# Two buffers for the last expert's first-layer weights in the space of the q tiles, between the q transposes and the combine weights

## The chip, the core and the metric

The kernel runs on one core of one Trainium2 chip. The core has TensorE (PE, matrix products into PSUM banks), VectorE (DVE), ScalarE (ACT), GpSimd (POOL) and SyncE (SP, which here only issues transfers), an on-chip memory of 128 partitions, and 16 DMA engines that all of SP's transfers share. The metric is the device time of one execution in microseconds; a kernel's time is the median of its runs.

## The reference

An attention with 32 memory slots per head feeds a mixture of eight experts that see only 4 slots each.

```python
# attention: batch 8, heads 8, seq 576, head_dim 64, n_mem 32
a = exp(phi - max(phi, axis=2)); a = a / (sum(a, axis=2) + 1e-9)
k_m = einsum('bhsm,bhsd->bhmd', a, k)
v_m = einsum('bhsm,bhsd->bhmd', a, v)
scores = q @ k_m.transpose(0, 1, 3, 2) / sqrt(64)
attn = softmax(scores, axis=-1)              # + 1e-9 in the divisor
x = (attn @ v_m).transpose(0, 2, 1, 3).reshape(4608, 512)
# experts: D 512, E 8, 4 slots per expert, F 1024
logits = x @ moe_phi                         # 4608 x 32
d = softmax over the 4608 rows; slot_input = (d.T @ x).reshape(8, 4, 512)
for e in range(8):
    slot_out[e] = maximum(slot_input[e] @ w1[e], 0) @ w2[e]
c = softmax over the 32 slots
out = c @ slot_out.reshape(32, 512)          # 4608 x 512, float32
```

The weights w1 and w2 are 16 MiB each, the inputs q, k and v 9 MiB each, phi 4.5 MiB and the output 9 MiB.

## The kernel before

The attention goes over the batch in four pairs. For each pair phi, k, v and q are loaded, the memory slots are formed (PE, L599), q is transposed in blocks of 32 by DVE (L700, two halves for each of the two batches, four instructions a pair), scores, softmax and logits follow, and `route` adds the pair's part to the experts' inputs. After the last pair the parts are combined into `SIM` (L1000), the input of all experts.

The experts come next. A weight load is 1 MiB: 2048 floats on each of 128 partitions. `expert_in` takes two such loads of w1 for each expert and multiplies `SIM` with them (L1064), `hidden` applies the maximum with 0 to four experts at once, transposes (L1089) and copies (L1095), `expert_out` takes two loads of w2 for each expert (L1113) and adds everything up in one PSUM bank. Between the experts of the second layer `slots` makes the combine weights c of one pair of batches: a softmax, a split into two float32r parts on DVE (L1158 and L1159, two of each), transposes on PE (L1170) and copies by ACT into `cT` (L1175). At last L1199 sums the four partial sums of the bank, ACT and DVE split the sum (L1204, L1207), L1220 multiplies it with cT for 36 blocks of 128 rows, ACT (L1229) and DVE (L1231) copy the results out of PSUM, and SP stores them (L1239) in 12 transfers of 768 KB.

Where things lie: most tiles of the attention share one arena of 44288 floats a partition. The weight buffers are cut from the same arena, 19 of them (`ws`, from `W0` up), so a weight load must wait until the attention tiles under its buffer are used up. The q tiles lie outside the arena, in a region of their own (`qtile`, two buffers of 2304 floats, `qs`). After the last q transpose cT takes that region.

What sets the order: each step is entered with `add`, with its engine, an assumed cost, what it reads and writes and a priority. A planner (`Plan.order`) plays the whole program through with these costs and writes each engine's instructions in the order in which they could start; on an engine other than SP it looks a little ahead and prefers low priority numbers. A pool (`Slots`) hands out buffers as the plan frees them, and its list `below` names pools over the same addresses that must be finished first. SP works off its queue strictly in order, and a transfer that waits for its buffer holds up all behind it. Each SP transfer adds to one of eight counters in turn, so that transfer n of the queue uses counter n modulo 8; a name such as DMAHW4_49 is a wait for such a counter, and PE_49 or DVE_49 one for an engine's.

Of the kernel before, what the change touches and what calls it, by code (L numbers as in the profile page):

```python
# [252 lines left out]
def kernel(  # L253
# [27 lines left out]
    E, DM, FF = w1.shape  # L281
# [41 lines left out]
    W_SZ = 2048  # L323
# [7 lines left out]
    CT_ALL = NBP * J * P  # L331
    TOP = 10 ** 6
    top_pool = ExitStack()
    qtile = top_pool.enter_context(tc.tile_pool(name="top", bufs=1)).tile([P, CT_ALL], F32, name="top")
# [3 lines left out]
    def shaped(off, shape):  # L338
        n = 1
        for x in shape:  # L340
            n *= x
        a = arena[:, off: off + n]
        if len(shape) > 1:
            names = "abcd"[: len(shape)]
            a = a.rearrange(
                f"p ({' '.join(names)}) -> p {' '.join(names)}",
                **dict(zip(names[:-1], shape[:-1])),
            )
        return a, (off, n)

    def area(off, shape, n, below=(), fifo=False):

        size = shaped(off, shape)[1][1]
        xs = [shaped(off + i * size, shape) for i in range(n)]
        return Slots([a for a, _ in xs], [r for _, r in xs], below, fifo)

    def stack(shape, n, fifo=False):
# [32 lines left out]
    qs = Slots(  # L390
        [qtile[:, i * Q_SZ: i * Q_SZ + Q_SZ] for i in range(2)],
        [(TOP + i * Q_SZ, Q_SZ) for i in range(2)], (), True,
    )
# [62 lines left out]
    def load(dst, src, nbytes, w, pri=None):  # L456
        add(
            SP, 0.06, lambda: nc.sync.dma_start(dst(), src), w=[w],
            dma=nbytes / DMA_RATE, pri=pri,
        )  # L460
# [465 lines left out]
    for bp in range(NBP):  # L926
# [14 lines left out]
        for h in range(2):  # L941
            plan.at(bp - 0.2 + 0.4 * h)
            for g in range(2):
                qt, t, f = hs[g][h]
# [77 lines left out]
    n_ct = NBP * J // G  # L1022
    NW = (ARENA - small) // W_SZ
    W0 = ARENA - NW * W_SZ
    ws = area(W0, [W_SZ], NW, early)
    ots = area(W0, [OT_SZ], NOUT, [ws])
    ct_tile = []

    def cT_view(i):
        if not ct_tile:  # L1030
            top_pool.close()
            pool = ctx.enter_context(tc.tile_pool(name="late", bufs=1, reuse_waits="tile"))
            ct_tile.append(pool.tile([P, CT_ALL], F32R, name="cT"))
        return ct_tile[0][:, i * CT_SZ: (i + 1) * CT_SZ]

    cTs = Slots(
        [(lambda i=i: cT_view(i)) for i in range(n_ct)], [(TOP, CT_ALL)] * n_ct, [qs],
    )


# [4 lines left out]
    hT = lambda: hTb.ap.rearrange("p (x y) -> p x y", x=8)  # L1045
    add(POOL, 2.0, lambda: nc.gpsimd.memset(hTb.ap, 0.0), r=[SIM], w=[hTb])

    def load_w(src):
        t = ws.tile()
        load(lambda: t.ap.rearrange("p (a x) -> p a x", a=src.shape[1]), src, 1 << 20, t)  # L1050
        return t

# [1 line left out]

    def expert_in(e, hb):
        w1v = w1[e].rearrange("(c p) f -> p c f", p=P)
        w1b = [load_w(w1v[:, 2 * i: 2 * i + 2]) for i in range(2)]
        for i in range(2):

            def f(i=i):  # L1060
                wv = w1b[i].ap.rearrange("p (c f) -> p c f", c=2)
                for c in range(2):
                    for j in range(4):
                        nc.tensor.matmul(  # L1064
                            hb.ap[NS * j: NS * j + NS, :256],
                            SIM.ap[:, 2 * i + c, NS * e: NS * e + NS],
                            wv[:, c, 256 * j: 256 * j + 256],
                            start=(e % EG == 0 and i == 0 and c == 0),
                            stop=(e % EG == EG - 1 and i == 1 and c == 1),
                            tile_position=(0, NS * j),  # L1070
                        )

            add(PE, pe(16, NS, 256, tiles=4), f, r=[SIM, w1b[i]], w=[hb])
# [138 lines left out]
    for bp in range(NBP):  # L1212
        for j0 in range(0, J, G):
            ot = ots.tile().split(G)
            for i in range(G):
                t = bp * J + j0 + i
# [59 lines left out]
```

## Time and profile before

| what | value |
|---|---|
| runs | 223.73 us median of 3 (223.68 to 225.53) |
| profiled execution | 221.83 us, of which its span is 220.1 us |
| PE busy | 172.5 us, 78% of the span |
| DVE busy | 135.5 us, 62% |
| ACT busy | 71.4 us, 32% |
| POOL busy | 86.7 us, 39% |
| transfers of SP's queue | 76.09 MB, 91.1% of 16 engines' span |
| weight loads | 32 of 1024 KB, 9.9 us median from issue to landing |

The span counts from the first to the last instruction of the execution; times inside it start at 0. Lines such as L700 are those of the kernel before. A row of the chain of waits has a start, a length and what ran; a row of the timeline has these with shapes and count, and in brackets how long the engine stood idle ahead of it and what ended that. A row of the windows has the stretch, its length, busy time of PE, PE's weight loads, DVE, ACT and POOL, then the granted TensorE clock (1.00 is full), the mean busy share of the DMA engines and what they moved in GB/s. Busy time is an average over stages with different limits, so the table alone doesn't say which engine sets the end.

### The profile page before, as it was taken

To read this page: it belongs to the slowest core of one execution; us is meant where nothing else is said; L and a number is where in the kernel's file an instruction comes from. 1 tells how busy PE (TensorE), PEld (TensorE's weight loads), DVE (VectorE), ACT (ScalarE), POOL (GpSimd) and SP (SyncE) were. 2 spreads that over 40 slices of the span, in tenths; PEclk is the share of its full clock that TensorE was granted. 3 is DMA by queue.
4 is the path that set the end of the run, shared out by engine and by line. 5 is a ranking of instruction groups with operands and counts; after the bars stand their busy time and mean duration, and the time that the engine had idled before them with its cause. 6 is when DMAs were issued, how large, how long until landed. Compare 5 with 4: busy or idle time off the path is not lost.

```text
span 220.1 us, 5624 instructions
## 1 busy us (share of the span) xinstructions
PE 172.5 (78%) x2418; PEld 105.3 (48%) x2418; DVE 135.5 (62%) x230; ACT 71.4 (32%) x182; POOL 86.7 (39%) x85
## 2 busy tenths in 40 slices
PE   8997977695798988598988799629999975599400
PEld 6676745354564654356654387415554340065100
DVE  6825048969459999879658965499102860268500
ACT  2041234542516626337342340201002331168400
POOL 6298019596934992999623641030000000000000
PEclk9999999979699999999969999976999999769755
DMA  6999999999999999999596493999999998049997
GB/s 215 383 395 390 380 392 381 390 380 390 385 388 389 388 406 380 389 392 406 194 410 212 188 420 102 401 350 327 395 413 410 408 409 320 3 179 411 415 415 295
DMA packets 27881, 76.45 MB, mean 347 GB/s; under 512 B 1744, under 2 KB 5840, under 8 KB 27856
## 3 DMA queue, kind: packets, MB, share of 16 engines
q1 hardware_dynamic: 27856, 76.09, 91.1%
q8 instruction: 19, 0.31, 0.6%
q14 instruction: 6, 0.05, 0.1%
HBM read 66.65 MB, written 9.44 MB: 346 GB/s over the span
## 4 chain that ended last, share of the span: by engine, by line
PE 41%; DMA 22%; DVE 14%; POOL 9%; issue 5%; ACT 2%; SPq 1%; DVEq 0%; POOLq 0%
DMA top<-in_q_dram 10%; DMA arena<-in_moe_w_dram 9%; PE bank L1064 7%; PE kvbank L476 6%; PE bank L785 5%; PE scbank L716 4%; PE bank L1220 4%; PE kvbank L599 3%; DMA out_dram<-arena 3%; DVE arena L700 3%; POOL arena L774 3%; POOL arena L562 3%; PE bank L849 2%; PE kvbank L1113 2%; POOL arena L751 2%
## 5 line engine op out<-in xcount | busy, mean ns | idle before, releaser
L549 POOL TENSOR_TENSOR arena<-arena 128x1152 f32<-128x1152 f32 x8 | 21.0, 2632 | 16.0 <-ACT arena L544 13.3
L476 PE MATMUL kvbank<-ones 128*128 128x256 f32 x92 | 25.4, 419 | 2.2 <-ACT arena L622 1.1
L700 DVE STREAM_TRANSPOSE arena<-top 128x1152 f32<-128x1152 f32 x16 | 21.7, 1361 | 7.1 <-DMA top<-in_q_dram 7.1
L774 POOL TENSOR_TENSOR arena<-arena,ssm 128x576 f32<-128x576 f32 x16 | 18.5, 1162 | 15.6 <-DVE ssm L770 15.5
L562 POOL TENSOR_TENSOR arena<-arena 128x128 f32<-128x128 f32 (+2 forms) x32 | 23.4, 731 | 2.3 <-ACT arena L555 0.3
L716 PE MATMUL scbank<-arena 64*64 64x288 f32 x256 | 21.6, 433 | 3.0 <-DVE arena L730 2.5
L785 PE MATMUL bank<-arena 128*128 128x288 f32 x64 | 21.4, 464 | 2.6 <-DVE arena L777 2.6
L751 POOL TENSOR_TENSOR arena<-arena,smx 128x576 f32<-128x576 f32 x16 | 18.4, 1158 | 11.5 <-DVE smx L746 11.5
L599 PE MATMUL kvbank<-arena 64*32 64x128 f32 x1152 | 20.2, 273 | 2.2 <-issue 1.5
L476 PEld LDWEIGHTS kvbank<-ones 128*128 128x128 f32 x92 | 18.1, 207 | 6.7 <-issue 1.6
L511 DVE TENSOR_REDUCE arena<-arena 128x128 f32<-128x1152 f32 x8 | 17.0, 2138 | 5.6 <-DMA arena<-in_phi_dram 5.6
L599 PEld LDWEIGHTS kvbank<-arena 64*32 64x32 f32 x1152 | 16.2, 106 | 6.3 <-issue 3.9
L1064 PE MATMUL bank<-arena,SIM 128*32 128x256 f32 x256 | 16.4, 421 | 3.4 <-DVE SIM L1000 3.4
L1113 PE MATMUL kvbank<-arena 128*32 128x512 f32 x128 | 15.6, 598 | 2.9 <-DMA arena<-in_moe_w_dram 2.9
L730 DVE STREAM_TRANSPOSE arena<-scbank 128x576 f32<-128x576 f32 x16 | 12.2, 765 | 8.9 <-PE scbank L716 8.9
L785 PEld LDWEIGHTS bank<-arena 128*128 128x128 f32 x64 | 12.1, 206 | 8.1 <-DVE arena L777 3.8
L1220 PE MATMUL bank<-sr,cT 128*128 128x512 f32 x36 | 13.2, 505 | 3.1 <-DVE sr L1207 1.4
L1231 DVE COPY arena<-bank 128x512 f32<-128x512 f32 x18 | 11.8, 691 | 4.7 <-DMA out_dram<-arena 2.4
L777 DVE STREAM_TRANSPOSE arena<-arena 128x576 f32<-128x576 f32 x16 | 12.1, 758 | 3.8 <-POOL arena L774 3.7
L716 PEld LDWEIGHTS scbank<-arena 64*64 64x64 f32 x256 | 9.0, 137 | 10.8 <-DVE arena L730 4.5
L756 ACT ACTIVATE arena<-arena 128x576 f32<-128x576 f32 x16 | 11.0, 688 | 8.4 <-POOL arena L751 8.4
L1064 PEld LDWEIGHTS bank<-arena,SIM 128*32 128x32 f32 x256 | 8.6, 121 | 10.7 <-DVE SIM L1000 3.6
(104 smaller groups left out, 234.4 us busy)
## 6 DMA issues: line engine op xcount, KB each, us to landing
arena<-in_moe_w_dram SPq DMA_DIRECT2D x32, 1024.0 KB, 9.9
top<-in_q_dram SPq DMA_DIRECT2D x8, 1152.0 KB, 13.8
arena<-in_k_dram SPq DMA_DIRECT2D x8, 1152.0 KB, 11.2
arena<-in_v_dram SPq DMA_DIRECT2D x8, 1152.0 KB, 13.6
out_dram<-arena SPq DMA_DIRECT2D x12, 768.0 KB, 7.6
arena<-in_phi_dram SPq DMA_DIRECT2D x8, 576.0 KB, 8.7
arena<-in_moe_phi_dram SPq DMA_DIRECT2D x1, 64.0 KB, 4.8
```

The lines of the kernel that those rows point to most:

```text
L476: lambda: nc.tensor.matmul(warm.ap, ones, ones.unsqueeze(1).to_broadcast([P, 2, P]), start=True, stop=True,),
L549: lambda: nc.gpsimd.tensor_tensor(ph(), ph(), mb.ap.unsqueeze(2).to_broadcast([P, C, J, M]), op=ALU.subtract),
L562: plus = lambda o, x, y: nc.gpsimd.tensor_tensor(o, x, y, op=ALU.add)
L599: nc.tensor.matmul(acc.ap[M * c: M * c + M, a, : 2 * D], ph()[h0: h0 + HALF, c, j, :], kv()[h0: h0 + HALF, :, c, j * D: j * D + D], start= ...
L700: nc.vector.transpose(qT.ap.rearrange("p (i u y) -> p u i y", i=2, y=Y), qt.ap[:, h * QT_SZ: h * QT_SZ + QT_SZ].rearrange("p (u i x) -> p ...
L716: nc.tensor.matmul(scb.ap[HALF * g: HALF * g + HALF, a, :JY], kb[g].ap[h0: h0 + HALF, i, c].rearrange("p r m -> p (r m)"), qT[g][c // 2].a ...
L751: lambda: nc.gpsimd.tensor_tensor(exv(), exv(), bc(mx), op=ALU.subtract),
L774: lambda: nc.gpsimd.tensor_tensor(exv(), exv(), bc(sm), op=ALU.mult),
L785: nc.tensor.matmul(lp.ap[:, :JY], vpb.ap[:, h, :], aT.ap[:, a * JY: (a + 1) * JY], start=(h == 0), stop=(h == H - 1),)
L1064: nc.tensor.matmul(hb.ap[NS * j: NS * j + NS, :256], SIM.ap[:, 2 * i + c, NS * e: NS * e + NS], wv[:, c, 256 * j: 256 * j + 256], start=(e ...
L1113: nc.tensor.matmul(pacc.ap[NS * x: NS * x + NS, 0, :DM], hT()[:, 4 * t + 2 * i + j, NS * e: NS * e + NS], wv[:, j, t, :], start=(e == 0 an ...
L1220: lambda po=po, i=i, ct=cT[bp, j0]: nc.tensor.matmul(po.ap[:, :DM], ct.ap()[:, i * P: i * P + P], sr.ap, start=True, stop=True),
```

## The change

A third pool of weight buffers, `wqs`, is cut from the q region: two buffers of 2048 floats at its start, to be had once the q tiles below them are done. They are used once each, for the two w1 loads of the last expert (e = 7). `cTs` now has to wait for `wqs` besides `qs`, since cT covers the same addresses.

```diff
     ots = area(W0, [OT_SZ], NOUT, [ws])
+    wqs = Slots(
+        [qtile[:, i * W_SZ: i * W_SZ + W_SZ] for i in range(2)],
+        [(TOP + i * W_SZ, W_SZ) for i in range(2)], [qs],
+    )
     ct_tile = []
...
     cTs = Slots(
-        [(lambda i=i: cT_view(i)) for i in range(n_ct)], [(TOP, CT_ALL)] * n_ct, [qs],
+        [(lambda i=i: cT_view(i)) for i in range(n_ct)], [(TOP, CT_ALL)] * n_ct, [qs, wqs],
     )
...
-    def load_w(src):
-        t = ws.tile()
+    def load_w(src, pool=ws):
+        t = pool.tile()
         load(lambda: t.ap.rearrange("p (a x) -> p a x", a=src.shape[1]), src, 1 << 20, t)
         return t
...
-        w1b = [load_w(w1v[:, 2 * i: 2 * i + 2]) for i in range(2)]
+        w1b = [load_w(w1v[:, 2 * i: 2 * i + 2], wqs if e == E - 1 else ws) for i in range(2)]
```

The four added lines move later line numbers by four: L1064 of before is L1068 after, L1170 is L1174.

SP's queue, from its transfer number 40 on (39 and all ahead of it stand as before; arena and top are the two regions, waits in brackets). Before:

```order
L458 DMA arena_67<-in_moe_w1_dram 128x2x1024 [waits DVE_49,DMAHW0_49,PE_49,DMAHW1_49,Activation_49,Pool_49]
L458 DMA arena_67<-in_moe_w1_dram 128x2x1024 [waits DMAHW2_49]
L458 DMA arena_67<-in_moe_w1_dram 128x2x1024
L458 DMA arena_67<-in_moe_w1_dram 128x2x1024 [waits DMAHW3_49,DVE_49,PE_49]
L458 DMA arena_67<-in_moe_w1_dram 128x2x1024 [waits DVE_49,DMAHW4_49,PE_49,Activation_49]
L458 DMA arena_67<-in_moe_w1_dram 128x2x1024 [waits DMAHW5_49]
L458 DMA arena_67<-in_moe_w1_dram 128x2x1024 [waits DMAHW6_49,DVE_49,PE_49]
L458 DMA arena_67<-in_moe_w1_dram 128x2x1024 [waits DMAHW7_49,DVE_49,PE_49]
L458 DMA arena_67<-in_moe_w1_dram 128x2x1024 [waits DMAHW0_49]
L458 DMA arena_67<-in_moe_w2_dram 128x2x1024 [waits DMAHW1_49,PE_49,Pool_49]
```

The same place after:

```order
L458 DMA top_71<-in_moe_w1_dram 128x2x1024 [waits DMAHW3_49,DMAHW0_49,DVE_49]
L458 DMA arena_67<-in_moe_w1_dram 128x2x1024 [waits PE_49,DMAHW1_49,Activation_49,Pool_49]
L458 DMA arena_67<-in_moe_w1_dram 128x2x1024 [waits DMAHW2_49]
L458 DMA arena_67<-in_moe_w1_dram 128x2x1024
L458 DMA top_71<-in_moe_w1_dram 128x2x1024 [waits DMAHW4_49,DVE_49]
L458 DMA arena_67<-in_moe_w1_dram 128x2x1024 [waits DMAHW5_49,PE_49]
L458 DMA arena_67<-in_moe_w1_dram 128x2x1024 [waits DMAHW6_49,PE_49,Activation_49]
L458 DMA arena_67<-in_moe_w1_dram 128x2x1024 [waits DMAHW7_49]
L458 DMA arena_67<-in_moe_w1_dram 128x2x1024 [waits DMAHW0_49,DVE_49,PE_49]
L458 DMA arena_67<-in_moe_w2_dram 128x2x1024 [waits DMAHW1_49,DVE_49,PE_49]
L458 DMA arena_67<-in_moe_w2_dram 128x2x1024 [waits DMAHW2_49]
L458 DMA arena_67<-in_moe_w2_dram 128x2x1024 [waits DMAHW3_49,PE_49,Pool_49]
```

The two loads into the q region stand as numbers 40 and 44, each behind a wait for DVE; the arena loads keep their waits one by one, and from the second on stand two numbers further down with them (the wait for PE and POOL of number 49 is now that of 51).

PE, from the eight instructions of the second layer that follow the second block's transposes to the sum L1199 (`kvbank` is the second layer's PSUM bank, `bank_62` to `bank_64` take the transposes of combine weights). Before:

```order
L1113 MATMUL kvbank<-arena 32x512 x8
L1170 MATMUL bank_63<-ident,arena 128x128 x3
L1170 MATMUL bank_64<-ident,arena 128x128 x3
L1113 MATMUL kvbank<-arena 32x512 x4
L1170 MATMUL bank_62<-ident,arena 128x128 x3
L1113 MATMUL kvbank<-arena 32x512 x4
L1170 MATMUL bank_63<-ident,arena 128x128 x3
L1170 MATMUL bank_64<-ident,arena 128x128 x3
L1170 MATMUL bank_62<-ident,arena 128x128 x3
L1113 MATMUL kvbank<-arena 32x512 x16
L1199 MATMUL bank_63<-arena,rep 128x512
```

The same place after:

```order
L1117 MATMUL kvbank<-arena 32x512 x16
L1174 MATMUL bank_63<-ident,arena 128x128 x3
L1174 MATMUL bank_64<-ident,arena 128x128 x3
L1174 MATMUL bank_62<-ident,arena 128x128 x3
L1117 MATMUL kvbank<-arena 32x512 x8
L1174 MATMUL bank_63<-ident,arena 128x128 x3
L1174 MATMUL bank_64<-ident,arena 128x128 x3
L1174 MATMUL bank_62<-ident,arena 128x128 x3
L1117 MATMUL kvbank<-arena 32x512 x8
L1203 MATMUL bank_63<-arena,rep 128x512
```

Four of these instructions use up one weight load; ahead of the third block's transposes there are now four loads' worth in place of two, and behind the fourth block's two in place of four. In the first layer the last sixteen instructions read the region `top` in place of the arena, with no other move.

ACT, from the copies of the first layer's results to the copies into cT, waits in brackets. Before:

```order
L1080 ACTIVATE arena<-bank_62 128x256 [waits PE_49,Activation_49]
L1080 ACTIVATE arena<-bank_64 128x256 [waits PE_49]
L1175 CAST cT<-bank_63 128x384 [waits DMAHW3_49,DMAHW4_49,DVE_49,PE_49]
L1175 CAST cT<-bank_64 128x384 [waits PE_49]
L1175 CAST cT<-bank_62 128x384 [waits DVE_49,PE_49]
```

The same place after:

```order
L1084 ACTIVATE arena<-bank_62 128x256 [waits PE_49,Activation_49]
L1084 ACTIVATE arena<-bank_64 128x256 [waits PE_49]
L1179 CAST cT<-bank_63 128x384 [waits DMAHW3_49,DMAHW0_49,DMAHW4_49,DVE_49,PE_49]
L1179 CAST cT<-bank_64 128x384 [waits PE_49]
L1179 CAST cT<-bank_62 128x384 [waits DVE_49,PE_49]
```

Nothing moves on ACT; the first copy into cT has one more counter to wait for, that of the first load into the q region.

## The prediction

> **What bounds the kernel now.** I read the page's slices first, then the chain of work that ended last, then windows of the DMA share, the queue's issues and the two engines that share the stage. The slices come first.
>
> ```profile
> DMA  6999999999999999999596493999999998049997
> GB/s 215 383 395 390 380 392 381 390 380 390 385 388 389 388 406 380 389 392 406 194 410 212 188 420 102 401 350 327 395 413 410 408 409 320 3 179 411 415 415 295
> ```
>
> A slice is 5.5 us. Transfers run without a pause to about 104 us, have holes from 104 to 138 us, run nearly without a pause again to 187 us, stop, and end with the output. So there is unused transfer time ahead of a stage that is full. The chain tells whether that stage sets the end.
>
> ```profile
> 147.67 10.18 PE bank L1064 x144
> ...
> 164.39 0.86 PE kvbank L1113 x8
> ...
> 168.59 18.81 DMA arena<-in_moe_w_dram
> 187.44 1.11 PE kvbank L1113 x8
> 188.58 0.70 DVE arena L1194
> 189.41 1.76 PE bank L1199 x2
> 191.20 0.59 ACT sr L1204
> 191.82 0.70 DVE sr L1207
> 192.57 7.80 PE bank L1220 x21
> 200.37 7.29 DMA out_dram<-arena
> ```
>
> It does: the last weight load, issued at 168.59, lands at 187.40; its eight matmuls end about 188.5 and everything after hangs on them in a row. The output that follows is itself full transfer time from its first tile on, so a shift of 188.5 shifts the end by as much.
>
> The windows say how large the holes are, and the transfer rate.
>
> ```profile
> 106.00:110.00 4.00, 3.58 (x66) 2.80 (x66) 2.06 (x4) 1.69 (x7) 2.20 (x2) 1.00 0.38 125
> 110.00:116.00 6.00, 5.34 (x33) 3.39 (x33) 3.30 (x7) 2.27 (x8) 1.16 (x1) 0.72 1.01 410
> 116.00:126.00 10.00, 8.23 (x106) 3.99 (x100) 9.48 (x18) 3.05 (x8) 4.95 (x5) 1.00 0.52 179
> 126.00:134.00 8.00, 8.00 (x48) 6.60 (x47) 5.52 (x9) 2.71 (x10) 4.22 (x4) 1.00 0.93 378
> 134.00:138.00 4.00, 3.54 (x16) 2.44 (x14) 1.41 (x3) 0.00 (x0) 0.00 (x0) 1.00 0.25 51
> 164.00:182.00 18.00, 16.87 (x146) 6.80 (x142) 9.47 (x24) 5.96 (x15) 0.00 (x0) 1.00 1.03 409
> ```
>
> The last two columns are DMA share and GB/s. From 164 to 182 us the rate is 409 GB/s, so one weight load of 1 MiB (1.049 MB) takes 1.049 / 0.409 = 2.56 us. From 116 to 126 us 48% of 10 us, 4.8 us, is unused, close to two loads.
>
> The issues of weight loads show why it is unused. Columns: start, time to the end of the group, count.
>
> ```profile
> 108.07 1.39 SPq L458 DMA_DIRECT2D arena<-in_moe_w_dram  x3
> 118.49 0.37 SPq L458 DMA_DIRECT2D arena<-in_moe_w_dram  x1
> 124.03 0.88 SPq L458 DMA_DIRECT2D arena<-in_moe_w_dram  x2
> 126.20 0.37 SPq L458 DMA_DIRECT2D arena<-in_moe_w_dram  x1
> 135.83 0.88 SPq L458 DMA_DIRECT2D arena<-in_moe_w_dram  x2
> 149.67 0.37 SPq L458 DMA_DIRECT2D arena<-in_moe_w_dram  x1
> ```
>
> SP waits for arena space that the attention still uses. Numbering SP's DMAs as they stand in its queue, 40 to 42 go at 108.07, 43 at 118.49, 44 and 45 at 124.03, 46 at 126.20, 47 and 48 at 135.83. The load at 149.67 is number 52, the first that waits for an expert matmul (L1064). From 52 to 64, 13 loads are left and nothing but the transfers paces them.
>
> **The change part by part.** Nothing is added or removed: 32 weight loads before and after, the same matmuls. Two loads, the last expert's two w1 halves, get a place outside the arena, and the 12 other loads that come after them in the queue each move into the arena space that stood two numbers earlier.
>
> *When the new places are free.* The first buffer (columns 0 to 2047) lies inside the first q buffer (0 to 2303), the second (2048 to 4095) over both. q buffers are read by L700, four times for the last pair, in turn; the third and the fourth end the use.
>
> ```profile
> 107.03 1.32 DVE L700 STREAM_TRANSPOSE arena<-top 128x1152 f32<-128x1152 f32 x1
> ...
> 111.82 1.37 DVE L700 STREAM_TRANSPOSE arena<-top 128x1152 f32<-128x1152 f32 x1
> ```
>
> So the first is free at 108.35, the second at 113.19. Queued behind the first is the group that went at 108.07: it goes about 0.8 us later (0.3 of wait, one issue of 0.4 to 0.5). Nobody reads those weights before L1064 begins at 147.67, and SP has no attention load left behind them, so this costs nothing; the cover is some 25 us.
>
> *What the transfers then do.* With 2.56 us a load and about 110.8 us as the start of data: loads 40 to 43 land by 121.1, 44 (issued 113.2) by 123.6, 45 (space of 118.49) by 126.2; 46 and 47 (space of 124.03) by 131.5; 48 (space of 126.20) by 134.1, as long as the old 46 took. The two extra loads fit the hole of 116 to 126 us. From 135.83 on SP stands two loads further: the load that waits for the first expert matmul at 149.67 is number 54, and 11 are left in place of 13. The last weight lands 2 x 2.56 = 5.1 us earlier, at 182.3. That the holes are used costs other engines nothing that the trace shows: L730 takes the same beside a full and beside a half-empty DMA.
>
> ```profile
> 91.66 0.78 DVE L730 STREAM_TRANSPOSE arena<-scbank 128x576 f32<-128x576 f32 x1
> ...
> 118.50 0.78 DVE L730 STREAM_TRANSPOSE arena<-scbank 128x576 f32<-128x576 f32 x1
> ```
>
> *What is late next.* PE, by its order. These are PE's and then DVE's rows at the end of the weights stage; in brackets the idle time ahead and its releaser.
>
> ```profile
> 178.40 1.06 PE L1113 MATMUL kvbank<-arena 128*32 128x512 f32 x8
> 180.47 1.17 PE L1170 MATMUL bank<-ident,arena 128*128 128x128 f32 x9 [1.00 <-DVE arena L1159]
> 181.57 1.92 PE L1113 MATMUL kvbank<-arena 128*32 128x512 f32 x16
> 184.97 1.06 PE L1113 MATMUL kvbank<-arena 128*32 128x512 f32 x8 [1.48 <-DMA arena<-in_moe_w_dram]
> 187.44 1.06 PE L1113 MATMUL kvbank<-arena 128*32 128x512 f32 x8 [1.40 <-DMA arena<-in_moe_w_dram]
> ...
> 178.52 0.45 DVE L1158 CAST arena<-arena 128x288 fp32r<-128x288 f32 x1
> ...
> 179.86 0.46 DVE L1159 TENSOR_TENSOR arena<-arena 128x288 fp32r<-128x288 f32 x1
> ```
>
> The trace counts eight records to a load. With data there, PE idles no more for the two DMA waits (1.48 and 1.40). The 1.00 us that it waited for DVE shrinks, because the new order has one more pair of loads ahead of the third block's transposes and only two loads behind the fourth's: the four DVE steps of the fourth block (178.52 to 180.32, 1.80 us) start when the third block's transposes end, about 179.35 by the sum of PE's work, and end 181.25; PE has two loads (1.92 us) to do meanwhile and waits some 0.15. Sum: 188.50 - 1.48 - 1.40 - 1.00 + 0.15 = 184.8; the last two loads, now on end, take the 1.92 of the row above rather than 2 x 1.06, 0.2 less, and a small seam between rows goes too: 184.5. The data would allow 182.3 + 1.1 = 183.4. So 5.1 us of earlier transfers are worth 4.0, since PE's own work takes the rest. The last copies to cT of the new order need about 0.5 us of ACT behind transposes that end 182.5, before PE is done: nothing.
>
> *The clock behind it.* After the last weights L1199 sums the parts, at a reduced clock.
>
> ```profile
> 186.30:189.70 3.40, 1.35 (x9) 0.46 (x10) 0.69 (x1) 0.00 (x0) 0.00 (x0) 1.00 0.03 13
> 189.70:193.10 3.40, 2.00 (x3) 0.50 (x2) 0.69 (x1) 0.59 (x1) 0.00 (x0) 0.50 0.02 5
> ...
> 131.07 2.79 PE kvbank L476 x12
> 192.57 3.78 PE L1220 MATMUL bank<-sr,cT 128*128 128x512 f32 x8 [1.40 <-DVE sr L1207]
> ```
>
> A stretch of 3.4 us with 1.35 us of PE work at clock 1.00 was followed by one at 0.50. After the change the 3.4 us ahead of the sum hold about 2.5 us of work, since the two DMA waits are gone. How L1199 goes at clock 1.00 no row shows; from L476 at 1.00, 2.79 / 12 = 0.23 us for 256 columns, I estimate 2 x 0.47 = 0.93 for its two of 512, against 1.76 now: 0.8 less. The first output tile needs three L1220, 3.78 / 8 = 0.47 each at 0.50, 0.7 less in all if that too went at 1.00. The ends are 0 (both as now) and -1.5 (both at 1.00); I take the sum at 1.00 and L1220 as now, -0.8, for the stretch ahead of L1220 stays thin (0.9 of about 3.2 us busy), like the 1.35 above.
>
> Sum against the profiled execution: 221.83 (span 220.1) - 4.0 - 0.8 = 217.0. The median of the runs is 223.73, 1.9 above that execution; the same 4.8 off it gives **218.9 us**.
>
> **The rivals.** *The clock as now.* It drops again ahead of L1199: 223.73 - 4.0 = 219.7. For it: the waits for DVE and ACT between L1199 and L1220 remain. Against it: the 2.5 us of work ahead.
>
> *The clock stays whole to the output.* 223.73 - 4.0 - 1.5 = 218.2. By the rows it needs the thin 3.4 us before L1220 to pass unseen, which the window at 186.3 did not. The Trainium skill (TensorE: Matmul & The Clock Gate, What's actually happening) has the gate fall to half only after at least one idle window of about 3.4 us; by that rule no gap here would be long enough. This trace doesn't agree, since 0.50 came behind a stretch with 1.35 us of work in it.
>
> *The hole isn't filled.* If the loads behind 40 and 44 fell back by what the two take, 13 loads' worth would still be open at 149.67, and the end stays: 223.7; with one load of two placed, DMA bounds the end, 2.56 us off, 221.2. For it: SP's queue is in order and two new waits for DVE stand in it. Against it: they end at 108.35 and 113.19, ahead of 118.49 and 124.03, so neither is the last wait.
>
> *The transposes wait (slower).* cT is laid over the same region, and its first copy now waits for the two loads also, on counters which every eighth DMA shares.
>
> ```profile
> 168.85 0.48 ACT L1175 CAST cT<-bank 128x384 fp32r<-128x384 f32 x1 [4.00 <-PE bank L1170]
> ```
>
> Were that wait to hold for the last load on such a counter (64, landing 182.3), PE would stop at the second block's transposes at 173.0, until the copy at 182.8, and end 184.5 + 9.8 = 194.3 rather than 188.5: 223.7 + 5.8 = 229.5. It decides once the first copy starts later than about 177. Against it: the copy waits today on counters 3 and 4, and load 60, the fifth from the end on counter 4, landed only about 187.40 - 4 x 2.56 = 177.2, yet the copy ran at 168.85. The waits are for a count reached long ago.
>
> **How the numbers follow.** Forecast 0.50; the clock as now 0.18; the clock whole 0.17; the hole not filled or half filled 0.11; transposes wait 0.04. Taking the first three and the half-filled case, low is 218.2 less 1.0 for a rate and runs that spread by 1.9 us before (221.83 to 223.73), 217.2; high is the half-filled 221.2. One per cent, 2.2 us, is about what a measurement can tell from no change: faster than 221.5 are the first three and a little of the fourth, 0.87; the same 0.09; slower 0.04.
>
> **What would show it.** Right: SP's issues near 108.4 and 113.2 into `top`, DMA share near 1 from 110 to 134 us, last weight landing near 182.3, no DMA wait ahead of the last expert matmuls or one below 0.3 us, their end near 184.5, L1199 near 0.9 us, the output's first issue 4 to 5.5 us earlier. Wrong: the last weight still near 187, arena issues after 118 us later than above, attention rows that grew beside the fuller DMA, or the first copy to cT later than 177.

## The result and the profile after

| comparison | kernel before | changed kernel | ratio, 95% interval |
|---|---|---|---|
| first | 224.63 us median of 4 | 220.26 us median of 4 (216.7 to 222.0) | 0.9713 [0.9645, 0.978] |
| second (`e1_again`) | 224.75 us median of 11 | 217.55 us median of 6 (216.24 to 221.01) | 0.9703 [0.9649, 0.9757] |
| third (`e9_again`) | 224.38 us median of 17 | 217.09 us median of 6 (216.77 to 219.42) | 0.9739 [0.9689, 0.9788] |

The change makes the kernel faster by 2.6 to 3.0%, 5.9 to 6.7 us of the times before. The medians are of all runs, while the ratios leave out disturbed ones; the first profiled execution of the changed kernel (222.0 us) was such a run, as were those of `e2_one`, `e6_before_tail` and `e8_gap_tail`, so the profile shown here is that of another execution, `e1_again` (216.24 us, span 214.5).

Its slices, 5.4 us each, with the DMA share in tenths and GB/s:

```profile
DMA  6999999999999999999969999498999998059997
GB/s 210 382 392 391 382 389 380 390 381 390 388 383 393 384 404 386 383 392 321 410 203 417 410 371 409 115 413 296 365 396 414 409 407 338 5 228 413 415 411 293
```

Of the holes in front of the experts' stage one is left at 107 us (203 GB/s) and one at 134 (115); the ones between are full (417, 410, 371, 409). The windows say it in numbers; the last two columns are DMA share and GB/s:

```profile
116.00:126.00 10.00, 8.24 (x110) 4.14 (x104) 8.98 (x17) 3.06 (x8) 4.98 (x5) 1.00 1.05 410
...
134.00:138.00 4.00, 3.86 (x17) 2.75 (x15) 1.69 (x4) 0.00 (x0) 0.00 (x0) 1.00 0.22 41
```

From 116 to 126 us the rate was 179 GB/s and is 410: 2.3 MB more in those 10 us, two loads and a little. Next the timeline, DVE's last three q transposes and then SP's issues (start, length, count):

```profile
107.55 1.36 DVE L700 STREAM_TRANSPOSE arena<-top 128x1152 f32<-128x1152 f32 x1
109.03 1.32 DVE L700 STREAM_TRANSPOSE arena<-top 128x1152 f32<-128x1152 f32 x1
113.81 1.36 DVE L700 STREAM_TRANSPOSE arena<-top 128x1152 f32<-128x1152 f32 x1
...
108.94 0.37 SPq L458 DMA_DIRECT2D top<-in_moe_w_dram  x1
110.09 1.40 SPq L458 DMA_DIRECT2D arena<-in_moe_w_dram  x3
115.21 0.37 SPq L458 DMA_DIRECT2D top<-in_moe_w_dram  x1
...
189.27 1.53 SPq L1243 DMA_DIRECT2D out_dram<-arena  x2
```

The two loads into `top` go 0.03 and 0.04 us after a transpose ends (108.91 and 115.17). The chain of waits shows what became of the end of the stage (here and below rows of issue, of at most 0.14 us, are left out):

```profile
148.19 9.97 PE bank L1068 x144
...
179.19 1.85 PE kvbank L1117 x16
...
181.17 1.17 PE bank L1174 x9
182.35 1.92 PE kvbank L1117 x16
184.29 0.70 DVE arena L1198
185.12 1.11 PE bank L1203 x2
...
187.63 6.12 PE bank L1224 x19
```

Before, a transfer of 18.81 us stood in it ahead of the last L1113. Now every step from the first expert matmul to the end of the weights is PE's: in this execution the transfers are no longer what ends last. When the last of them lands can be read from the rate between 160 and 195 us, in slices of 0.875 us:

```profile
GB/s 417 421 421 403 417 412 417 412 412 403 431 384 403 407 417 403 403 417 398 421 403 417 403 389 155 47 0 0 0 19 0 0 0 0 267 407 414 421 400 421
```

Next to nothing moves after the 26th slice, which ends at 182.75; before, the last weight landed at 187.40. Not every execution goes this way. In the first profile of the changed kernel the clock was 0.50 from 142.3 to 155.9 us, the experts began at 150.93, and the last weight landed at 187.68, no earlier than before.

The time splits into three parts that can be read from the chain and the issues of any execution. The stage is from the first expert matmul to the end of the last, the tail from there to the first issue of an output transfer:

| us | before | `e1_again` | difference |
|---|---|---|---|
| first expert matmul | 147.67 | 148.19 | +0.5 |
| stage | 40.9 (to 187.44 + 1.11) | 36.1 (to 182.35 + 1.92) | -4.8 |
| tail | 6.3 (to 194.87) | 5.0 (to 189.27) | -1.3 |
| span | 220.1 | 214.5 | -5.6 |

The three differences make up the -5.6 of the span, so the output itself takes as long as before. The runs' -5.9 to -6.7 is a little more; 5.6 lies inside each of the three intervals.

### The profile page after: what moved, and what is told of

It reads as the page before. It is cut to its first block, busy times and chain, and to the rows that moved or that the text cites. A ratio compares the mean times of both kernels' runs of the same rounds, so it can differ in the third digit from the quotient of the medians.

```text
span 220.2 us, 5622 instructions
## 1 busy us (share of the span) xinstructions
PE 178.6 (81%) x2418; PEld 109.5 (50%) x2418; DVE 134.1 (61%) x230; ACT 71.3 (32%) x182; POOL 86.6 (39%) x85
## 4 chain that ended last, share of the span: by engine, by line
PE 42%; DMA 22%; DVE 13%; POOL 9%; issue 6%; ACT 3%; SPq 1%; DVEq 0%; POOLq 0%
DMA top<-in_q_dram 10%; DMA arena<-in_moe_w_dram 9%; PE bank L1068 8%; PE kvbank L476 6%; PE bank L785 5%; PE scbank L716 5%; PE kvbank L599 3%; PE bank L849 3%; PE bank L1224 3%; DMA out_dram<-arena 3%; DVE arena L700 3%; POOL arena L562 3%; POOL arena L774 3%; POOL arena L751 2%; DVE arena L511 2%
## 5 line engine op out<-in xcount | busy, mean ns | idle before, releaser
L476 PE MATMUL kvbank<-ones 128*128 128x256 f32 x92 | 25.8, 424 | 2.2 <-ACT arena L622 1.1
L700 DVE STREAM_TRANSPOSE arena<-top 128x1152 f32<-128x1152 f32 x16 | 21.6, 1357 | 7.4 <-DMA top<-in_q_dram 7.4
L716 PE MATMUL scbank<-arena 64*64 64x288 f32 x256 | 22.7, 450 | 3.0 <-DVE arena L730 2.5
L476 PEld LDWEIGHTS kvbank<-ones 128*128 128x128 f32 x92 | 18.2, 209 | 7.2 <-issue 2.0
L730 DVE STREAM_TRANSPOSE arena<-scbank 128x576 f32<-128x576 f32 x16 | 12.3, 768 | 8.4 <-PE scbank L716 8.4
L1117 PE MATMUL kvbank<-arena 128*32 128x512 f32 x128 | 15.2, 597 | 1.2 <-DMA arena<-in_moe_w_dram 1.2
L1068 PE MATMUL bank<-arena,SIM 128*32 128x256 f32 x224 | 15.0, 433 | 1.2 <-DVE SIM L1000 1.2
L1224 PE MATMUL bank<-sr,cT 128*128 128x512 f32 x36 | 13.0, 504 | 3.1 <-DVE sr L1211 1.4
L716 PEld LDWEIGHTS scbank<-arena 64*64 64x64 f32 x256 | 9.5, 141 | 10.7 <-DVE arena L730 4.0
L761 DVE TENSOR_REDUCE ssm<-arena 128x18 f32<-128x576 f32 x16 | 11.5, 723 | 2.0 <-ACT arena L756 2.0
```

The lines of the kernel that those rows point to most:

```text
L476: lambda: nc.tensor.matmul(warm.ap, ones, ones.unsqueeze(1).to_broadcast([P, 2, P]), start=True, stop=True,),
L700: nc.vector.transpose(qT.ap.rearrange("p (i u y) -> p u i y", i=2, y=Y), qt.ap[:, h * QT_SZ: h * QT_SZ + QT_SZ].rearrange("p (u i x) -> p ...
L716: nc.tensor.matmul(scb.ap[HALF * g: HALF * g + HALF, a, :JY], kb[g].ap[h0: h0 + HALF, i, c].rearrange("p r m -> p (r m)"), qT[g][c // 2].a ...
L1068: nc.tensor.matmul(hb.ap[NS * j: NS * j + NS, :256], SIM.ap[:, 2 * i + c, NS * e: NS * e + NS], wv[:, c, 256 * j: 256 * j + 256], start=(e ...
L1224: lambda po=po, i=i, ct=cT[bp, j0]: nc.tensor.matmul(po.ap[:, :DM], ct.ap()[:, i * P: i * P + P], sr.ap, start=True, stop=True),
```

## The experiments

All ratios are to the kernel before on the same chip; of `e5_one_again` there is one run and so no ratio. Stage and tail are those of the one profiled execution; they are left out for the three named above.

| label | kernel | median, us | ratio, 95% interval | stage | tail |
|---|---|---|---|---|---|
| `e1_again` | the change | 217.55 of 6 | 0.9703 [0.9649, 0.9757] | 36.1 | 5.0 |
| `e2_one` | one buffer | 220.41 of 7 | 0.9825 [0.9766, 0.9885] | | |
| `e3_late` | both, used late | 221.37 of 6 | 0.9853 [0.9793, 0.9912] | 40.9 | 6.6 |
| `e4_fill` | the change, 14 fillers more | 219.2 of 6 | 0.9795 [0.9745, 0.9845] | 35.5 | 5.0 |
| `e5_one_again` | one buffer | 221.32 of 1 | | 39.7 | 5.0 |
| `e6_before_tail` | before, fillers in the tail | 224.58 of 12 | 1.001 [0.9966, 1.0053] | | |
| `e7_gap` | the change, 3 fillers in a wait | 217.45 of 6 | 0.9743 [0.9701, 0.9784] | 36.7 | 5.0 |
| `e8_gap_tail` | e7, fillers in the tail | 219.02 of 6 | 0.9715 [0.9669, 0.9761] | | |
| `e9_again` | the change | 217.09 of 6 | 0.9739 [0.9689, 0.9788] | 36.3 | 5.0 |
| `e10_before_tail2` | before, fillers in the tail, other bank | 223.94 of 12 | 0.9935 [0.9882, 0.9989] | 40.9 | 5.1 |
| `e11_memset` | the change, hT cleared by DVE | 217.18 of 6 | 0.975 [0.969, 0.981] | 37.0 | 5.7 |
| `e12_memset_tail` | e11, fillers in the tail | 215.97 of 6 | 0.9658 [0.9612, 0.9704] | 37.1 | 5.0 |

A filler is one of the matmuls of `ones` (L476) that the kernel runs only to keep TensorE busy.

**The change once more.** No edit, for a profile and a closer ratio; the third comparison repeats it beside other kernels.

> The changed kernel as it is, for another profile: in the first one the clock was 0.50 from 142.25 to 155.91 us and the last weight landed at 187.6, no earlier than before. Theory (two loads fill the hole of 116 to 126 us, and a longer stretch of half clock hid that in the first profile): with the clock back at 1.00 by about 152 us, as in the profile of before, the last weight lands 182 to 183, the expert matmuls end 184 to 185, the span is 214.5 to 216. Rival (the weights land no earlier whatever the clock does, and the gain of the runs comes from the clock alone): the last weight lands 187 to 188 again while the span is below 217.

> The change once more, to stand beside the three others on one chip: 0.966 to 0.977 of the kernel before. In its profile the time from the first expert matmul to the end of the last is 36 to 38 us (before 40.8).

Measured: 0.9703 and 0.9739, stages of 36.1 and 36.3 us, tails of 5.0 us in both. The parts are steady; the two profiles differ by when the experts start (148.19 and 148.66).

**One buffer in place of two.** The first w1 load of the last expert goes to `top`, the second to the arena.

```diff
-        [qtile[:, i * W_SZ: i * W_SZ + W_SZ] for i in range(2)],
-        [(TOP + i * W_SZ, W_SZ) for i in range(2)], [qs],
+        [qtile[:, i * W_SZ: i * W_SZ + W_SZ] for i in range(1)],
+        [(TOP + i * W_SZ, W_SZ) for i in range(1)], [qs],
...
-        w1b = [load_w(w1v[:, 2 * i: 2 * i + 2], wqs if e == E - 1 else ws) for i in range(2)]
+        w1b = [load_w(w1v[:, 2 * i: 2 * i + 2], wqs if e == E - 1 and i == 0 else ws) for i in range(2)]
```

> One buffer in the q region instead of two, for the first w1 load of the last expert only; the other stays in the arena. Theory: one load of 2.56 us moves into the hole, 12 loads are left at the first expert matmul instead of 13 or 11, the last weight lands 184.8 to 185.2 beside 187.4 before, and the data sets the end again: the expert matmuls end about 186.2, 2.3 us earlier than before, about half of what two buffers give; time 2.3 to 3.8 us below before with the clock term. Rival (clock or order alone): as far below before as with two buffers.

> One buffer again, for a profile without the long half clock that its first profile had from 141.2 to 154.9 us. Theory: the last weight lands about 185.0 to 185.4 (182.9 with two buffers and 187.4 with none, in profiles whose clock was back by 152 us), and the expert matmuls end when it has landed plus 1.1 us. Rival (the new order or the clock alone makes the gain): 187 or later.

Measured: 0.9825 [0.9766, 0.9885], some 3.9 us off where two buffers take 6.7; the two intervals do not touch. The timeline of PE in `e5_one_again`, its last expert matmuls:

```profile
185.75 1.07 PE L1117 MATMUL kvbank<-arena 128*32 128x512 f32 x8 [0.31 <-DMA arena<-in_moe_w_dram]
188.25 1.06 PE L1117 MATMUL kvbank<-arena 128*32 128x512 f32 x8 [1.43 <-DMA arena<-in_moe_w_dram]
```

PE still waits for both of the last two loads: with one buffer the transfers remain the bound, and only the second buffer hands it to PE (in `e1_again` and `e9_again`). But the last weight lands at 188.21, where 185.0 to 185.4 was expected; 187 or later was the sign of the rival. The windows of the same execution say where the gain went:

```profile
110.00:116.00 6.00, 4.92 (x29) 3.56 (x29) 3.66 (x7) 2.20 (x9) 1.34 (x2) 0.79 0.93 341
116.00:126.00 10.00, 8.23 (x88) 4.20 (x94) 8.19 (x15) 3.30 (x9) 3.71 (x5) 0.95 0.80 311
...
138.00:144.00 6.00, 3.94 (x42) 1.73 (x41) 2.87 (x7) 1.53 (x7) 0.00 (x0) 0.74 0.92 349
144.00:152.00 8.00, 6.00 (x44) 4.27 (x48) 4.85 (x15) 0.71 (x4) 2.02 (x1) 0.50 0.65 228
```

From 116 to 126 us the transfers gain 132 GB/s on the kernel before, 1.3 MB or 3.2 us, and 0.2 MB more from 106 to 110. They lose as much around it: 69 GB/s from 110 to 116, 57 from 138 to 144 and 106 from 144 to 152 (before 410, 406 and 334), 1.6 MB in all. The stage of 39.7 us is 1.1 shorter than before only because the experts start 1.95 later (149.62); the last weight lands 0.8 later than before, and the span is 0.6 shorter by the tail alone. So this profile, with the clock at 0.50 from 140.9 to 154.5 us, does not show the worth of one load. For that only the ratio of `e2_one` counts; how much of its 3.9 us (2.6 to 5.3) is transfer and how much tail, no run here splits.

**Both buffers, but not before the hole is over.** The loads into `top` are made to wait in the plan for `SIM`, so that they stand as numbers 51 and 52 of the queue. The same addresses and the same number of buffers, without the early issue.

```diff
-    def load(dst, src, nbytes, w, pri=None):
+    def load(dst, src, nbytes, w, pri=None, r=()):
         add(
-            SP, 0.06, lambda: nc.sync.dma_start(dst(), src), w=[w],
+            SP, 0.06, lambda: nc.sync.dma_start(dst(), src), r=r, w=[w],
...
-        load(lambda: t.ap.rearrange("p (a x) -> p a x", a=src.shape[1]), src, 1 << 20, t)
+        load(lambda: t.ap.rearrange("p (a x) -> p a x", a=src.shape[1]), src, 1 << 20, t,
+             r=[SIM] if pool is wqs else ())
```

> Both buffers, but their two loads stand in SP's queue as numbers 51 and 52, behind the load that goes near 144 us, instead of 40 and 44; the hole of 116 to 126 us stays empty. Theory (what counts is transfer time that lay idle): only the smaller holes from 144 to 152 us are filled, by sum 2.3 us; the last weight lands about 185.1, the expert matmuls end about 186.2. Rival (two buffers more, 21 instead of 19, are what counts, loaded at whatever time): as early as with the change, 182 to 183.

Measured: 0.9853 [0.9793, 0.9912], slower than the change by 1.5% of the time before, with intervals apart. Its windows, and then its chain:

```profile
116.00:126.00 10.00, 8.24 (x106) 3.99 (x100) 9.52 (x18) 3.06 (x8) 4.99 (x5) 1.00 0.55 173
...
144.00:152.00 8.00, 4.60 (x49) 2.08 (x48) 7.53 (x18) 0.45 (x1) 2.02 (x1) 0.60 0.99 361
152.00:164.00 12.00, 12.00 (x218) 6.81 (x214) 2.69 (x8) 0.83 (x2) 0.00 (x0) 0.98 1.02 408
```

```profile
167.64 18.88 DMA arena<-in_moe_w_dram
186.56 1.98 PE kvbank L1118 x8
```

The hole of 116 to 126 us is as empty as before (173 GB/s, before 179), and a transfer is back in the chain. The last weight lands at 186.52; 185.1 was expected. The size was wrong, for the windows of the kernel before leave little to fill so late:

```profile
144.00:152.00 8.00, 4.60 (x50) 2.06 (x50) 7.53 (x18) 0.44 (x1) 2.02 (x1) 0.58 0.95 334
152.00:164.00 12.00, 12.00 (x219) 6.76 (x215) 2.73 (x8) 0.83 (x2) 0.00 (x0) 0.99 1.00 391
```

27 GB/s more over 8 us and 17 over 12 are 0.42 MB, at 409 GB/s 1.0 us; the last weight came 0.9 us earlier. What the ratio gives beyond that (3.3 us, 2.0 to 4.7) this profile does not show: its last matmuls ran at half clock (1.98 for eight in place of 1.1). That remainder stays open. The plan also keeps PE's old order in this kernel, with the third block's nine transposes in two parts (176.24 and 178.02); but that order does not set the end where, as here and before, a transfer ends last.

**More fillers ahead of the first expert matmul.** Is the gain one of clock rather than of transfers? From 144 to 152 us, where the experts start, the granted clock is 0.58 before and 0.59 in `e1_again`. With 14 fillers more it is 1.00.

```diff
-    NTAIL = 12
+    NTAIL = 26
```

> The change with 26 instead of 12 filler matmuls (L476, nobody reads them); the 14 more stand on PE from the last logits to the first expert matmul, 0.47 us each at full clock. Theory (thin PE work from 138 to 147 us halves the clock for the first expert matmuls and, in some runs, for route ahead of them): the clock stays 1.00 from 126 to 185 us, the first 60 expert matmul records take about 3.3 us instead of 5.6, arena space comes free earlier, the expert matmuls end 1 to 2.5 us earlier than in a run of the change with half clock only from 145 to 152, and runs scatter less. Rival (the fillers stand in the way): up to 1.8 us later, since 1 to 1.5 us of filler lie in gaps of 0.4 to 1.2 us; the first expert matmul starts after 149.5.

```profile
151.17 7.98 PE bank L1068 x144
...
166.65 18.81 DMA arena<-in_moe_w_dram
185.51 1.11 PE kvbank L1117 x8
```

The chain of `e4_fill`: the 144 matmuls take 7.98 us in place of 9.97, but start at 151.17 in place of 148.19. The stage is 0.6 us shorter than the change's, but the start is 3.0 later, and PE waits for a transfer again: the last weight lands at 185.46. The ratio 0.9795 says that the fillers cost about 2 us more than the clock is worth; the two intervals overlap by a little (0.9745 to 0.9757). The clock of the first layer is not where the change's gain is: it is the same before and after, and to raise it in this way gained nothing.

**Three fillers in PE's wait for SIM.** The cheaper form of the same, in the 3.4 us that PE stands idle ahead of the first expert matmul.

```diff
+    NGAP = 3
...
+    fill(NGAP, FILL + 1, [sip])
     m4 = keep("m4", [P, NS])
```

> The change with three filler matmuls in PE's wait of 3.4 us between the last route matmuls and the first expert matmul, where they stand in nobody's way. Theory (thin PE work there halves the clock for the first expert matmuls): half clock after 145 us becomes shorter or rarer, the first expert matmul starts no later than with the change (148.2), the stage from there to the last expert matmul takes up to 0.6 us less than its 36.1, and runs scatter less; 0 to 1 us below the change, 217.55. Rival (fillers cost): 1 us or more above it, as with 14 fillers (219.2).

Measured: 0.9743 [0.9701, 0.9784] against 0.9703 and 0.9739 of the change, which were taken on other chips: no gain can be told. Its chain:

```profile
149.77 9.89 PE bank L1070 x144
...
166.47 18.82 DMA arena<-in_moe_w_dram
```

The first 144 matmuls took 9.89 us, so the clock was at half all the same. And a transfer ends last, at 185.29. The experts start 1.1 us later than in `e9_again`, because the clock was at half from 140.1 to 143.4 us already, ahead of the fillers (36 matmuls of L850 took 3.01 us; 1.67 in `e9_again`). From 138 to 144 and from 144 to 152 us the transfers moved 333 and 286 GB/s, in `e9_again` 369 and 329. So with the change the last weight and PE's own work lie close together: PE ends last in the profiles where the experts start by 148.7 us, a transfer in those where they start at 149.8 or later (`e7_gap`, `e8_gap_tail`, `e4_fill`, the first profile). That the later start is the cause is read from these profiles; no run moves it alone.

**The tail's clock, without the change.** The prediction's smaller term says that the sum and the first output tiles go faster where TensorE was busier ahead of them. Fillers in the kernel before do that alone: two behind the last expert matmul, three behind the sum.

```diff
+    fill(2, FILL + 1, [pacc])
+    fill(3, FILL + 1, [so])
     for bp in range(NBP):
```

> The kernel before with two filler matmuls (L476, nobody reads them) between the last expert matmul and the sum L1199 and three between the sum and the first L1220; nothing else. Theory (the change wins 4.2 us in the weights stage, and 1.5 us behind it because the two waits for data that let the clock fall ahead of the sum are gone): the last weight still lands 187 to 188; the clock that the first output tile sees is higher in part of the runs, 0 to 1.3 us below before, since the waits for data in front of the sum stay. Rival (most of the change's gain is the clock): 3 us or more below before.

Measured: 1.001 [0.9966, 1.0053]. The chain shows why that settles nothing:

```profile
192.44 0.64 PE kvbank L476 x2
193.11 0.70 DVE arena L1194
```

The fillers write into `kvbank`, the bank that L1194 reads, and the copy starts 0.64 us late behind them; whether the hardware or the program's own dependences hold it back, no run tells apart. The same pair added to `e7_gap`:

> The change with the three fillers of the run before it and with the fillers ahead of and behind the sum as in the run on the kernel before. Theory: behind the change PE already runs the sum and the first output matmuls at full clock in most runs, so the fillers at the end bring 0 to 0.6 us more, by the runs where it does not; the output's first issue stands 4.8 us behind the last expert matmul, as in the change's second profile (184.27 to 189.09). Rival: the fillers delay sum and output, 0.5 us or more behind the run with the gap's fillers alone.

Measured: 0.9715 [0.9669, 0.9761], not to be told from `e7_gap` by the ratio, and with the same fault; its median is 1.6 us higher, since three of the six runs lie at 220.7 to 220.9. The next kernel has the fillers write to a score bank, which nobody uses by then:

```diff
+    warm2 = Tile(ap=scbank[:, 1, 256:512])
+
-    def fill(n, pri, r=()):
+    def fill(n, pri, r=(), warm=warm):
...
+    fill(2, FILL + 1, [pacc], warm2)
+    fill(3, FILL + 1, [so], warm2)
     for bp in range(NBP):
```

> The kernel before with two fillers ahead of the sum and three behind it as in the earlier run, but written into the bank of the scores, so that the copy L1194 doesn't wait for them (it did by 0.64 us). Theory (part of the change's gain is that the sum and the first output tiles run at full clock, 1.6 us by the two profiles): the first output issue stands 4.7 to 5.2 us behind the last expert matmul beside 6.4 in the profile of before, L1199 takes 1.1 us beside 1.76; 0.7 to 1.6 us below before, the rest of the change's gain is not there. Rival (the clock behind the weights is worth nothing in most runs): within 0.4 us of before.

```profile
188.75 1.06 PE scbank L478 x4
189.81 0.96 PE bank L1201 x2
```

The chain of `e10_before_tail2`: the sum takes 0.96 us in place of 1.76 and the tail 5.1 in place of 6.3, while the stage stays at 40.9. The ratio 0.9935 [0.9882, 0.9989] makes that 1.5 us, 0.2 to 2.6. So a tail at whole clock is worth some 1.3 us by itself in the profile, which is the size by which the change's tail is shorter; the runs confirm it only roughly.

**The wait of 1.9 us ahead of SIM.** L990, a small step of DVE, takes about 1.9 us in eight of the twelve profiles with the clearing on POOL, while POOL clears `hT` (L1046 before). Here DVE clears it, after its own work for `SIM`.

```diff
-    add(POOL, 2.0, lambda: nc.gpsimd.memset(hTb.ap, 0.0), r=[SIM], w=[hTb])
+    add(DVE, 1.5, lambda: nc.vector.memset(hTb.ap, 0.0), r=[SIM], w=[hTb], pri=10 ** 5)
```

> The change, with the clearing of the hidden layer's tile (2304 floats a partition) on DVE behind the combine weights' first steps instead of on POOL. In the profiles of before and of the change's second run L990, a DVE step on the path to the first expert matmul, took 1.90 us while POOL cleared that tile, and 0.18 us where it ran ahead of the clearing. Theory (the clearing blocks L990): L990 takes 0.2 us, the first expert matmul starts up to 1.7 us earlier, 0.7 to 1.7 us below the change itself. Rival (the start of the expert matmuls doesn't set the end, the transfers do): L990 is short and the time as with the change.

```profile
145.80 0.18 DVE L990 TENSOR_SCALAR st<-st 128x32 f32<-128x32 f32 x1
```

and from the chain of the same execution the first output tiles:

```profile
187.55 7.58 PE bank L1224 x21
```

L990 falls to 0.18 us and the first expert matmul starts at 147.23, 1.4 earlier than in `e9_again`. Yet the ratio is 0.975 [0.969, 0.981], no better than the change's, where 0.7 to 1.7 us less was expected: the first 144 matmuls take 10.88 us in place of 10.22, more of them at half clock, and the stage and the tail are each 0.7 longer. In the tail the clock fell to half from 187.3 to 190.7 us, and L1224 went slower (7.58 us for 21 records, in `e1_again` 6.12 for 19). With the tail's fillers (in the score bank, as above) added:

> The change with the clearing on DVE and the five fillers at the end (in the bank of the scores). Theory: as the run with the clearing alone, and in the runs where the clock fell ahead of the sum up to 1.5 us less; 215 to 216.5 us, fewer runs above 218. Rival: the fillers cost 0.3 us or more.

Measured: 215.97 us, 0.9658 [0.9612, 0.9704]. It has the shortest span (213.8) and the lowest ratio of all, though the interval still overlaps that of the change in the same comparison (0.9739 [0.9689, 0.9788]), and two of its six runs lie above 218 us (218.63 and 220.11; of the change's six one, 219.42), where fewer were expected. A lead over the change is likely, not shown.

## Why the prediction was right

The forecast was 218.9 us, -4.8 on the profiled execution. The profile after shows -5.6, the ratios -5.9 to -6.7, and the medians are 220.26, 217.55 and 217.09, the last just under the low end of 217.2. In `e1_again` and `e9_again` the mechanism went as the prediction has it, from the hole to PE's order; three sizes were off. That it went so far took an early start of the experts: the prediction has no term for a later one, and in the first profile, `e4_fill` and `e7_gap`, where they start 2.1 to 3.5 us later than before, a transfer ended last.

*When the new places are free.* Right for the second, off for the first, without harm. The first buffer is free with the end of the second L700 (108.91), not of the third (110.35) as the prediction took it. The group behind it went at 110.09 by its own waits.

*What the transfers do.* Right in these two: 410 GB/s from 116 to 126 us, the last weight by 182.75 (predicted 182.3, with experts that start 0.5 later here). That the early issue into this hole counts, and not only the place outside the arena, `e3_late` shows: the same two buffers without it lose 3.4 us of the 6.7. Of the other half its profile accounts for about 1 us, and the rest is open. That both loads count shows the ratio of `e2_one`, which loses 2.7. So the rival of a hole that isn't filled fell.

*That a fuller DMA costs other engines nothing.* L730 beside the full transfers took 0.78 us (at 116.92), as before. The experts started at 148.19 and 148.66 in the two profiles, at 147.67 before; but the first of the q transposes shown stood at 107.55 already, 2.7 later than its like before (104.83), ahead of any load that the change moved. So this half microsecond is not the fuller DMA's. Why that transpose stands at 105.9 to 107.6 in every profile of a kernel with the early issue, and at 104.7 to 104.8 in those of before, `e3_late` and `e10_before_tail2`, no run shows.

*What is late next.* Right in these two: PE by its order. Its timeline in `e1_again`, and under it that of the kernel before at the like place:

```profile
179.12 1.92 PE L1117 MATMUL kvbank<-arena 128*32 128x512 f32 x16
181.17 1.17 PE L1174 MATMUL bank<-ident,arena 128*128 128x128 f32 x9
```

```profile
176.15 0.84 PE L1170 MATMUL bank<-ident,arena 128*128 128x128 f32 x6
176.93 1.07 PE L1113 MATMUL kvbank<-arena 128*32 128x512 f32 x8
177.93 0.55 PE L1170 MATMUL bank<-ident,arena 128*128 128x128 f32 x3
```

No wait for a transfer is left, and of the wait for DVE 0.13 us (in the chain the row at 179.19 ends at 181.04, the next starts at 181.17) where 0.15 was forecast. The term that was mis-sized is what the prediction called two loads on end and a small seam, 0.3 in all. From the first eight L1117 (164.71) to the end PE took 19.6 us, before (164.39 to 188.55) 24.2: 4.6 less, of which the three waits are 3.9 - 0.13. The other 0.85 is work that runs on in longer rows: up to the third block's end 32 matmuls and nine transposes took 5.37 us in five rows (174.10 to 179.47) and take 4.71 in two (174.41 to 179.12), and the last sixteen matmuls take 1.92 where twice eight took 2.12. With 0.2 from the first layer the stage is 4.8 shorter in place of 4.0.

*The clock behind it.* The step that put L1220 "as now" failed in these two profiles; the rival of the clock that stays whole (-1.5, chance 0.17) came true there in place of it. The windows of `e1_again`:

```profile
182.90:186.30 3.40, 2.42 (x16) 0.46 (x10) 0.69 (x1) 0.12 (x2) 0.00 (x0) 1.00 0.02 5
186.30:189.70 3.40, 2.07 (x7) 1.19 (x7) 2.00 (x4) 1.98 (x4) 0.00 (x0) 1.00 0.00 0
```

In each trace the times at which the granted clock changes lie a whole number of 3.41 us apart, as if on marks (before at 111.2, 114.7, 145.4, 152.1, 189.8 and 196.5; in `e1_again` at 145.5, 152.3 and 200.0), and the two windows begin and end within 0.1 us of such marks. The prediction's 2.5 us of work ahead of the sum are there (2.50 from 181.72 to 185.12), but that is not the stretch between two marks: the first window's 2.42 include the sum itself. The stretch ahead of L1224 was taken for thin, 0.9 us busy; as the marks fell, the second window holds the start of L1224 too and comes to 2.07, and the clock stayed.

Where the marks fall was luck. In `e11_memset` the tail's rows lie within 0.1 us of these, but its marks lie at 183.9 and 187.3; the stretch between them holds 1.37 us of work, as the 1.35 before, and the clock fell. In the first profile it fell too: the sum took 1.67 us and the tail 6.2, about as before. In `e1_again` the sum took 1.11 us (0.93 forecast), the first output tiles went at whole clock, and the tail was 1.3 shorter in place of 0.8. `e10_before_tail2` measured the same term alone: 1.3 in its profile, 1.5 by its ratio (0.2 to 2.6). So the rival of the clock as now fell for `e1_again` and `e9_again`, not for every execution.

*The transposes wait.* Fell. The first copies into cT on ACT's timeline:

```profile
169.16 1.25 ACT L1179 CAST cT<-bank 128x384 fp32r<-128x384 f32 x3 [4.00 <-PE bank L1174]
```

They start at 169.16 and wait for PE alone, not for a load; it would have had to be later than 177.

So the sum reads +0.5 - 4.8 - 1.3 where it was forecast as 0 - 4.0 - 0.8.

## What to carry to other kernels

Unused transfer time counts only if a load can be placed in it: look for a region that falls free just before the hole and gets its next user long after, and count how far every load behind moves up in the queue. Once the transfers no longer end last, the gain is cut off by the next order, here PE's, so walk through that engine's rows with the waits taken out and with pieces that join up measured as joined. Then ask how far the two bounds lie apart: here, in the profiles where the experts started 1 to 3 us later, a transfer ended last again. A shorter wait can also keep the clock up behind it, though here that turned on where the clock's marks fell; that term can be measured alone by a few fillers in the kernel before, provided they write to a bank that nobody is about to read.

## What the runs showed of the hardware

**A clearing on POOL holds up DVE.** The timelines of the kernel before and of the first profiled execution of the changed one:

```profile
144.38 2.02 POOL L1046 MEMSET arena<- 128x2304 f32 x1 [11.25 <-PE bank L909]
144.53 1.90 DVE L990 TENSOR_SCALAR st<-st 128x32 f32<-128x32 f32 x1
```

```profile
149.82 2.02 POOL L1050 MEMSET arena<- 128x2304 f32 x1 [13.99 <-PE bank L909]
149.51 0.18 DVE L990 TENSOR_SCALAR st<-st 128x32 f32<-128x32 f32 x1
```

DVE's step of 32 columns takes 0.18 us when it starts ahead of the clearing and 1.90 when it starts behind it, up to within 0.03 us of the clearing's end (146.43 and 146.40). The Trainium skill (SBUF — State Buffer, SBUF: two separate sides) describes a port pair that DVE in some modes and GpSimd share as an exclusive lock, for the whole of the instruction that came first; the rows agree, with an instruction on POOL that only writes.

**The clock falls without an idle stretch, and changes on marks.** Windows of the kernel before, whose ends lie within 0.1 us of marks at which the granted clock can change:

```profile
107.80:111.20 3.40, 2.44 (x31) 2.06 (x22) 2.08 (x6) 0.70 (x3) 0.55 (x1) 1.00 0.55 187
111.20:114.60 3.40, 3.28 (x9) 2.28 (x9) 2.13 (x4) 0.99 (x6) 1.16 (x1) 0.50 1.02 420
...
182.90:186.30 3.40, 1.66 (x16) 0.16 (x8) 0.00 (x0) 0.00 (x0) 0.00 (x0) 1.00 0.85 341
```

Half clock follows 2.44 us of PE work in 3.4, with less than 1 us idle in all, while the stretch behind 1.66 us of work (186.30 to 189.70) is at whole clock. So the busy time of a stretch alone does not tell which way the clock goes, and it is a term to bound from both sides. How long half clock lasts differs too: one step of 3.4 us here, two in `e1_again` (145.5 to 152.3), four in the first profile (142.3 to 155.9).
